# A conv and MLP-mixer kernel on one core: products of the turning tiles as pairs of 64-row halves, crossed between two banks

## The chip, the core and the metric

The kernel runs on one core of a Trainium2 chip. PE (TensorE) does the matrix products, ACT (ScalarE) and DVE (VectorE) the elementwise work, POOL and SP mostly start DMA transfers. The metric is the device time of one launch in microseconds. PE ran at its full granted clock in every slice of the profile of before.

## What is computed

Eight batches of 4096 tokens by 192 channels. A causal convolution of seven taps comes first, its taps per head softmaxed (`wsm`); then an MLP-mixer block with its two residual sums:

```python
w = np.exp(weight - weight.max(-1, keepdims=True)); w /= w.sum(-1, keepdims=True) + 1e-09
x = np.einsum('hk,bskhg->bshg', w, x_unf)                  # 7 shifted copies of x
h = np.maximum(x.transpose(0, 2, 1) @ w_tok1, 0.0) @ w_tok2    # 4096 -> 256 -> 4096 tokens
u = x + h.transpose(0, 2, 1)
out = u + np.maximum(u @ w_ch1, 0.0) @ w_ch2                   # 192 -> 1536 -> 192 channels
```

The kernel computes in fp32, mostly with operands split in a high and a low part of type fp32r (`hi`, `lo`), of which three of the four products are taken (high by high, high by low, low by high). Where fp32 itself is used a product runs as two passes.

## The kernel before

The batches form the groups [0], [1], [2, 3], [4, 5], [6, 7]. For each group the token mixing has two parts. Mix part 1 (`mix`, L929, the products at L938 or L942 to L944) sums over all 4096 tokens into two accumulator banks `ps_a0` and `ps_a1`, one for each half `kc` of the 256 mixed tokens; it runs in the background while the group before is still in its channel MLP. A planner, `bg`, keeps lists of background items with a cost, a lag and a gate, and pops them when the foreground calls `bg.fg` with the time that its last products took; while `bg.tiled` is set it pops no products. In group 1 (one batch) mix part 1 is fp32 with 192 columns, in the two-batch groups fp32r with 384.

The foreground goes tile by tile, 512 tokens of one batch each. A tile is four blocks of 128 tokens (`j`). Per tile PE does:

- **channel1** (L1261): 108 products of 64 rows by 512 columns. Two halves of the array work at a time, rows 0 to 63 on one bank and rows 64 to 127 on another: a pair. `bg.tiled` is set. ACT makes `hh` (L1315) and DVE `hl` (L1320) from each bank.
- **mix2** of the next tile, if this is a *turning* tile, the last of its tile's batches: whole 128-row products, one bank for each block j (L1109, L1110 with one batch: 384 and 192 columns; L1112 to L1114 with two: 384 columns each). DVE adds the bank to `u` (L1124, L1125 or L1128).
- **channel2**: on a turning tile `channel2`, whole rows, one bank a block, 12 steps f with an `hh` product of 384 columns (L1369) and an `hl` product of 192 (L1370), then two adds a block (L1375, L1376). On other tiles `channel2_halves` (L1337): the same in pairs of row halves, each half with its own bank, and four adds a block (L1343, L1345).
- the next tile's `u` must be turned so that the channels lie on partitions. With one batch PE transposes it (`transposed_once`, L1183, 8 transposes a tile in the middle of channel2); with two, DVE turns 32 by 32 blocks (`turn_blocks`, L1150), DMA sends them to their places (`blocks_sent`, L1201, queues of SP and POOL), ACT copies what returns (`parted`, L1213) and swaps the row halves (L1218).

Some two-batch tiles have time to be mixed a tile ahead (`spread`): their mix2 is `mix2_half` (L1139), in pairs, woven into `channel2_halves`. It is used where the background has no products left. So PE goes between pairs and whole rows at the turning tiles: pairs in channel1, whole rows in mix2 and channel2, and pairs again in the next channel1. The order of each engine is what the code writes, in the order in which `bg` pops.

## Time and profile before

| | before |
|---|---|
| median of 3 runs | 2005.86 us (2005.25 to 2006.46) |
| profiled execution, device time | 2004.13 us |
| its span, first to last instruction | 2002.4 us |
| PE busy | 1995.6 us (100%), 19007 products |
| DVE busy | 1507.4 us (75%) |
| ACT busy | 788.9 us (39%) |

Busy time counts an instruction from start to end. PE's instructions overlap in its pipeline, so how long a product takes is the step from one start to the next, not its length. In a timeline each row is the start, the length, engine, line, operation, output and inputs, shape and count; `64*128` is a half-row product, `128*128` a whole one. `[0.16 <-X]` is idle time ahead of the instruction, and what ended it.

### The profile page before, as it was taken

Reading aid. Unit: us, or ns where it says so; the run is one execution under the profiler, and the core shown is the slowest. Engines: PE = TensorE matmul, PEld = TensorE weight load, DVE = VectorE, ACT = ScalarE, POOL = GpSimd, SP = SyncE. Lnnn points to the kernel's source line nnn. Section 1 sums busy time; section 2 is a strip of 40 time slices with the busy share of each in tenths; the row PEclk is TensorE's granted clock in tenths of the full one; section 3 lists DMA queues with packets and bytes.
Section 4 is the critical chain, followed back from the end, with each engine's and each line's share of the span. In section 5 each row is a group of like instructions: output and inputs, shape, how many; then the busy total and the mean of one; then the engine's idle time right before and its main releaser. Section 6 shows DMA issues by size and latency. Waiting matters only on the chain.

```text
span 2002.4 us, 45321 instructions
## 1 busy us (share of the span) xinstructions
PE 1995.6 (100%) x19007; PEld 1852.3 (93%) x19007; DVE 1507.4 (75%) x3021; ACT 788.9 (39%) x1312; POOL 212.6 (11%) x374
## 2 busy tenths in 40 slices
PE   9999999999999999999999999999999999999999
PEld 9899999999989999999999999999999999999998
DVE  6999989999569999747898789556666666666664
ACT  7668544444343343423333433323333322333322
POOL 1000000010011101111111110111111110011110
PEclk9999999999999999999999999999999999999999
DMA  9956555553365365524346543533322222333310
GB/s 302 297 151 218 172 164 170 177 195 128 114 173 151 112 190 175 158 72 132 84 129 184 139 142 107 132 88 85 86 71 76 75 67 59 80 86 85 86 49 17
DMA packets 282080, 259.26 MB, mean 129 GB/s; under 512 B 190100, under 2 KB 231924, under 8 KB 281876
## 3 DMA queue, kind: packets, MB, share of 16 engines
q1 hardware_dynamic: 258180, 172.75, 30.6%
q0 software_dynamic: 22608, 82.97, 13.8%
q8 instruction: 150, 2.46, 0.5%
q10 hardware_dynamic: 1088, 0.64, 0.1%
q14 instruction: 54, 0.44, 0.1%
HBM read 147.25 MB, written 71.30 MB: 109 GB/s over the span
## 4 chain that ended last, share of the span: by engine, by line
PE 97%; DMA 1%; DVE 1%; POOL 0%; ACT 0%; SPq 0%; issue 0%; POOLq 0%; DVEq 0%
PE ps_x L1261 39%; PE ps_x L1337 26%; PE ps_x L1369 12%; PE ps_x L1370 5%; PE ps_x L1139 3%; PE ps_a L942 2%; PE ps_a L943 2%; PE ps_a L944 2%; PE ps_x L1109 1%; PE ps_a L938 1%; PE ps_x L1112 1%; PE ps_x L1281 1%; DMA x<-in_x_dram 1%; PE ps_x L1114 1%; PE ps_x L1113 1%; DMA dec_raw<-in_moe_w_tok_dram 1%
## 5 line engine op out<-in xcount | busy, mean ns | idle before, releaser
L1315 ACT ACTIVATE hh<-ps_x 128x512 fp32r<-128x512 f32 x752 | 408.7, 596 | 844.3 <-PE ps_x L1261 844.2
L1320 DVE SCALAR_TENSOR_TENSOR hl<-ps_x,hh 128x512 fp32r<-128x512 f32 x752 | 482.5, 685 | 177.9 <-ACT hh L1315 177.2
L1337 PE MATMUL ps_x<-w,hh 64*128 64x384 f32 x3648 | 523.0, 355 | 0.0
L1337 PE MATMUL ps_x<-w,hl 64*128 64x192 f32 x3648 | 458.4, 247 | 0.0
L1261 PE MATMUL ps_x<-other,w_hi 64*128 64x512 f32 x1728 | 448.3, 388 | 0.0
L836 DVE SCALAR_TENSOR_TENSOR xc<-raw,cw,xc 128x384 f32<-128x384 f32 (+1 forms) x768 | 388.5, 561 | 4.6 <-ACT xc L834 4.5
L1337 PEld LDWEIGHTS ps_x<-w,hl 64*128 64x128 f32 x3648 | 351.0, 188 | 1.5
L1261 PE MATMUL ps_x<-own_hi,w_hi 64*128 64x512 f32 x1440 | 346.3, 391 | 0.7 <-ACT w_hi L674 0.4
L1337 PEld LDWEIGHTS ps_x<-w,hh 64*128 64x128 f32 x3648 | 344.8, 184 | 1.5
L1261 PEld LDWEIGHTS ps_x<-other,w_hi 64*128 64x128 f32 x1728 | 315.2, 184 | 32.2 <-DVE hl L1320 0.4
L1261 PE MATMUL ps_x<-own_hi,w_lo 64*128 64x512 f32 x1440 | 341.9, 387 | 0.0
L1261 PE MATMUL ps_x<-own_lo,w_hi 64*128 64x512 f32 x1440 | 341.2, 386 | 0.0
L1369 PE MATMUL ps_x<-w,hh 128*128 128x384 f32 x1172 | 339.5, 360 | 0.0
L1370 PE MATMUL ps_x<-w,hl 128*128 128x192 f32 x1176 | 294.4, 250 | 0.0
L1261 PEld LDWEIGHTS ps_x<-own_lo,w_hi 64*128 64x128 f32 x1440 | 218.4, 184 | 25.5 <-DVE own_lo L1170 0.2
L1261 PE MATMUL ps_x<-other,w_lo 64*128 64x512 f32 x864 | 242.0, 386 | 0.0
L1261 PEld LDWEIGHTS ps_x<-own_hi,w_lo 64*128 64x128 f32 x1440 | 218.1, 184 | 25.6 <-DVE w_lo L675 0.2
L1261 PEld LDWEIGHTS ps_x<-own_hi,w_hi 64*128 64x128 f32 x1440 | 213.7, 184 | 29.4 <-issue 4.3
L1370 PEld LDWEIGHTS ps_x<-w,hl 128*128 128x128 f32 x1176 | 224.5, 191 | 0.0
L1369 PEld LDWEIGHTS ps_x<-w,hh 128*128 128x128 f32 x1172 | 220.1, 188 | 0.4 <-DVE hl L1320 0.4
L1345 DVE TENSOR_TENSOR osb<-ps_x,osb 128x192 f32<-128x192 f32 x456 | 163.1, 358 | 27.9 <-DVE osb L1345 1.8
L1261 PEld LDWEIGHTS ps_x<-other,w_lo 64*128 64x128 f32 x864 | 159.0, 184 | 16.9
(212 smaller groups left out, 2049.3 us busy)
## 6 DMA issues: line engine op xcount, KB each, us to landing
raw<-in_x_dram SPq DMA_DIRECT2D x56, 672.0 KB, 8.0
t<-t2d SPq DMA_DIRECT2D x64, 512.0 KB, 5.3
out_dram<-osb POOLq DMA_DIRECT2D x61, 384.0 KB, 4.2
xcd<-xc POOLq DMA_DIRECT2D x28, 768.0 KB, 7.7
u<-xcd SPq DMA_DIRECT2D x56, 384.0 KB, 5.5
t<-t1p SPq DMA_DIRECT2D x32, 512.0 KB, 6.1
other<-own_hi POOLq DMA_DIRECT2D x24, 384.0 KB, 3.9
other<-own_lo POOLq DMA_DIRECT2D x24, 384.0 KB, 3.8
```

What stands on the lines that cost most here:

```text
L836: nc.vector.scalar_tensor_tensor(out=dst, in0=src, scalar=cw[:, h, k:k + 1], in1=dst, op0=ALU.mult, op1=ALU.add)
L942: nc.tensor.matmul(out=ps, lhsT=wh, rhs=xh, start=a, stop=False)
L943: nc.tensor.matmul(out=ps, lhsT=wh, rhs=xl, start=False, stop=False)
L944: nc.tensor.matmul(out=ps, lhsT=wl, rhs=xh, start=False, stop=z)
L1139: nc.tensor.matmul(out=ps[:, :n], lhsT=t2[ks, kc, r, j, :], rhs=h1[ks, kc, v, :n], start=m == 0, stop=m == len(prods) - 1)
L1261: nc.tensor.matmul(out=ps, lhsT=w1[w][rows, chunks[h][c], p * P:(p + 1) * P], rhs=t[h][v][rows, c], start=n == 0, stop=n == len(prods) - 1,)
L1315: nc.scalar.activation(out=h["hh", f], in_=ps, func=AF.Relu)
L1320: nc.vector.scalar_tensor_tensor(out=h["hl", f], in0=ps, scalar=0.0, in1=f32(h["hh", f]), op0=ALU.max, op1=ALU.subtract)
L1337: nc.tensor.matmul(out=ps[:, :m], lhsT=h[part, f][ks, ts], rhs=w2[ks, f, :m], start=n == 0 and part == "hh", stop=z and part == "hl",)
L1345: nc.vector.tensor_tensor(out=osb[:, j], in0=v, in1=osb[:, j], op=ALU.add)
L1369: nc.tensor.matmul(out=ps[:, :2 * D], lhsT=h["hh", f][:, ts], rhs=w2[:, f, :], start=n == 0, stop=False)
L1370: nc.tensor.matmul(out=ps[:, :D], lhsT=h["hl", f][:, ts], rhs=w2[:, f, :D], start=False, stop=z)
```

## The change

Four kinds of products that were whole become pairs of row halves that are *crossed* between two banks: mix2 of the groups after the first (`crossed`, after's L463), mix part 1 (after's L1004), the transposes (after's L1276) and channel2 of every tile that isn't spread, save the last tile (`channel2_crossed`, after's L1474). For two blocks `one` and `two`, the first step takes rows 0 to 63 of `one` into the bank of `one`, beside rows 64 to 127 of `two` into the bank of `two`; a later step takes the other halves, so that each bank ends with the whole sum, and two adds a block suffice. The order of the steps over a tile's four blocks is `CROSSED`: (0, 1), (2, 3), then (1, 0) and (3, 2). Group 0's mix2 stays in whole rows, and so do the first tile's products and the last tile's channel2.

A bank's second half must come after its first. This is ordered through ScalarE: `signal` issues an empty ScalarE instruction (`nop`), which waits for PE's first halves, and PE's first product of the second half waits for that. The adds of mix2 come after the third and the fourth step, two blocks each; mix part 1 is split in two parts (`part` 0 and 1), taken for two `q` one after the other, with a gate on part 1. The core of the diff:

```diff
+    def signal():
+        if unsignalled:
+            relay = nc.scalar.nop(nofuse=True)
+            for key in unsignalled:
+                ordered(relay, tops_of[key][1])
+                tops_of[key] = tops_of[key][0], relay
+            unsignalled.clear()
+
+    def crossed(outs, prods, one, two, part):
+        for n, js in enumerate(zip(prods(one), prods(two))):
+            for r, (j, (m, lhs, rhs)) in enumerate(zip((one, two), js)):
+                rs = slice(r * D2, (r + 1) * D2)
+                z = len(prods(j)) - 1
+                mm = nc.tensor.matmul(
+                    out=outs[j][:, :m], lhsT=lhs(rs), rhs=rhs(rs), start=part == 0 and n == 0, stop=part == 1 and n == z
+                )
+                row_tile((id(outs), j), r, mm, part and not n, not part and n == z)
+
+    def row_tile(ps, r, mm, first, last):
+        if first and r != tops_of.get(ps, (r,))[0]:
+            ordered(mm, tops_of[ps][1])
+        if last:
+            tops_of[ps] = r, mm
+            unsignalled.append(ps)
+
+    CROSSED = ((0, 1, 0), (2, 3, 0), (1, 0, 1), (3, 2, 1))
...
-        def mix(q2, q, kc):
+        def mix(q2, q, part):
...
+            way = (q // 2 + part) % 2
+            if way != crossing["way"] and any((id(accs), kc) in unsignalled for kc in range(KC)):
+                signal()
...
+            for n in range(len(made[0])):
+                for r in range(2):
+                    kc = (r + way) % 2
+                    rs = slice(r * D2, (r + 1) * D2)
+                    m, lhs, rhs = made[kc][n]
+                    mm = nc.tensor.matmul(
+                        out=accs[kc][:, :m], lhsT=lhs(rs), rhs=rhs(rs), start=first_way and n == 0,
+                        stop=last_way and n + 1 == len(made[0]),
+                    )
+                    row_tile((id(accs), kc), r, mm, not n, n + 1 == len(made[0]))
...
+            if q % 2 == 0:
+                it.gate = lambda: 0.0 if bg.finishing or (id(accs), 0) not in unsignalled else None
@@ mix2, for the groups after the first @@
+        for one, two, part in CROSSED:
+            if not part:
+                for j in (one, two):
+                    pss[j] = ps_x.tile([P, TT], F32, name="ps_x")
+            crossed(pss, prods, one, two, part)
+            signal()
+            bg.fg(570 if nb == 1 else 1040, 2 * (660 if nb == 1 else 600) if part else 0, 200)
+            if part:
+                for j in (two, one):
+                    added(j, pss[j])
@@ transposed_once @@
+        def turned(part):
             for j in range(TJ):
-                nc.tensor.transpose(out=ps[:, j * P:(j + 1) * P], in_=cols, identity=ident)
+                for r in range(2):
+                    rs, c = slice(r * D2, (r + 1) * D2), (r + part) % 2
+                    cols = u[rs, j].rearrange("p c b d -> p (c b d)")[:, c * D2:(c + 2) * D2]
+                    mm = nc.tensor.transpose(out=pss[c][:, j * P + r * D2:j * P + (r + 1) * D2], in_=cols, identity=ident[rs, rs])
...
+    def channel2_crossed(i, h, u, osb, at, tiled):
...
+        for k, (one, two, part) in enumerate(CROSSED):
...
+            for n in range(0, 2 * NF, 8):
+                z = n + 8 == 2 * NF
+                for m in range(n, n + 8):
+                    for r, j in enumerate((one, two)):
+                        rs = slice(r * D2, (r + 1) * D2)
+                        w, lhs, rhs = made[j][m]
+                        mm = nc.tensor.matmul(
+                            out=pss[j][:, :w], lhsT=lhs(rs), rhs=rhs(rs), start=not part and m == 0,
+                            stop=part == 1 and m + 1 == 2 * NF,
+                        )
+                        row_tile((id(pss), j), r, mm, part and not m, not part and m + 1 == 2 * NF)
+                        if m % 8 == 1 and r:
+                            signal()
+                bg.fg(1140, 1320 if z and part else 0, 200)
+                if (k, n // 8) in at:
+                    at[k, n // 8]()
+            if part:
+                for j in (two, one):
+                    ps = pss[j]
+                    nc.vector.tensor_tensor(out=rows(osb[:, j]), in0=rows(ps[:, :D]), in1=tokens(u, i)[:, j], op=ALU.add)
+                    nc.vector.tensor_tensor(out=osb[:, j], in0=ps[:, D:2 * D], in1=osb[:, j], op=ALU.add)
```

PE's order at mix2 of the first two-batch tile, before. `ps_x_...` is a bank, `h1` and `t2` the operands; `[waits ...]` names the semaphores of the engines or DMA queues that an instruction waits for.

```order
L1112 MATMUL ps_x_6566<-h1_481,t2_6408 128x384 [waits DMAHW3_49,DVE_49]
L1113 MATMUL ps_x_6566<-h1_481,t2_6408 128x384
L1114 MATMUL ps_x_6566<-h1_481,t2_6408 128x384
L1112 MATMUL ps_x_6566<-h1_481,t2_6408 128x384 [waits DMAHW4_49,Activation_49]
L1113 MATMUL ps_x_6566<-h1_481,t2_6408 128x384
L1114 MATMUL ps_x_6566<-h1_481,t2_6408 128x384
L1112 MATMUL ps_x_6575<-h1_481,t2_6408 128x384 [waits DVE_49]
L1113 MATMUL ps_x_6575<-h1_481,t2_6408 128x384
```

The same place after: two banks in turn in each step, and the second halves begin with a wait on the ScalarE relay.

```order
L463 MATMUL ps_x_8496<-h1_481,t2_8338 128x384 [waits DMAHW3_49,DVE_49]
L463 MATMUL ps_x_8497<-h1_481,t2_8338 128x384 [waits DVE_49]
L463 MATMUL ps_x_8496<-h1_481,t2_8338 128x384
...
L463 MATMUL ps_x_8511<-h1_481,t2_8338 128x384 [waits DVE_49]
L463 MATMUL ps_x_8512<-h1_481,t2_8338 128x384 [waits DVE_49]
L463 MATMUL ps_x_8511<-h1_481,t2_8338 128x384
...
L463 MATMUL ps_x_8497<-h1_481,t2_8338 128x384 [waits Activation_sequencer_49]
L463 MATMUL ps_x_8496<-h1_481,t2_8338 128x384
L463 MATMUL ps_x_8497<-h1_481,t2_8338 128x384
L463 MATMUL ps_x_8496<-h1_481,t2_8338 128x384
```

Every product is now half as high and there are twice as many; the bank of a block is written in two steps, which lie one step apart.

PE's order where the background's mix part 1 stands behind a block of mix2, in a tile of the groups of two batches, before:

```order
L1112 MATMUL ps_x_8933<-h1_481,t2_8357 128x384 [waits DMAHW6_49]
L1113 MATMUL ps_x_8933<-h1_481,t2_8357 128x384
L1114 MATMUL ps_x_8933<-h1_481,t2_8357 128x384
L942 MATMUL ps_a0_6757<-xhl_8385,t1_8137 128x384
L943 MATMUL ps_a0_6757<-xhl_8385,t1_8137 128x384
L944 MATMUL ps_a0_6757<-xhl_8385,t1_8137 128x384
L942 MATMUL ps_a0_6757<-xhl_8385,t1_8137 128x384
```

and after, where mix part 1 takes the accumulators the other way round than the time before:

```order
L463 MATMUL ps_x_11249<-h1_481,t2_10656 128x384
L463 MATMUL ps_x_11250<-h1_481,t2_10656 128x384
L463 MATMUL ps_x_11249<-h1_481,t2_10656 128x384
L463 MATMUL ps_x_11250<-h1_481,t2_10656 128x384
L1004 MATMUL ps_a0_8811<-xhl_10476,t1_8839 128x384 [waits Activation_sequencer_49]
L1004 MATMUL ps_a1_8812<-xhl_10476,t1_8839 128x384
L1004 MATMUL ps_a0_8811<-xhl_10476,t1_8839 128x384
```

The first product of mix part 1 now waits for a relay that stands right behind the step of mix2 ahead of it.

PE's order in group 0's mix2, where a background product of group 1 stands behind a block, before:

```order
L1109 MATMUL ps_x_1853<-h1_481,t2s_1652 128x384 [waits Activation_49]
L1110 MATMUL ps_x_1853<-h1_481,t2s_1652 128x192
L938 MATMUL ps_a0_778<-xc0_1092,t1_942 128x192 [waits DMAHW1_49]
L938 MATMUL ps_a0_778<-xc0_1092,t1_942 128x192
L938 MATMUL ps_a1_779<-xc0_1092,t1_942 128x192 x2
L1109 MATMUL ps_x_1871<-h1_481,t2s_1652 128x384 [waits DVE_49]
L1110 MATMUL ps_x_1871<-h1_481,t2s_1652 128x192
```

and after:

```order
L1201 MATMUL ps_x_2069<-h1_481,t2s_1856 128x384 [waits Activation_49]
L1201 MATMUL ps_x_2069<-h1_481,t2s_1856 128x192
L1004 MATMUL ps_a0_778<-xc0_1092,t1_942 128x192 [waits DMAHW1_49]
L1004 MATMUL ps_a1_779<-xc0_1092,t1_942 128x192
L1004 MATMUL ps_a0_778<-xc0_1092,t1_942 128x192
L1004 MATMUL ps_a1_779<-xc0_1092,t1_942 128x192
L1201 MATMUL ps_x_2084<-h1_481,t2s_1856 128x384 [waits DVE_49]
L1201 MATMUL ps_x_2084<-h1_481,t2s_1856 128x192
```

Mix part 1's products are half-row pairs on both accumulators there, with whole rows ahead and behind.

## Rows read from the trace of the kernel before

**Rows 1.** The page: busy time of each engine, and the chain's shares by engine.

```profile
PE 1995.6 (100%) x19007; PEld 1852.3 (93%) x19007; DVE 1507.4 (75%) x3021; ACT 788.9 (39%) x1312; POOL 212.6 (11%) x374
...
PE 97%; DMA 1%; DVE 1%; POOL 0%; ACT 0%; SPq 0%; issue 0%; POOLq 0%; DVEq 0%
```

**Rows 2.** PE's timeline from channel1 to channel2_halves, 598 us: start, length.

```profile
598.29 0.39 PE L1261 MATMUL ps_x<-own_lo,w_hi 64*128 64x512 f32 x1
...
598.52 0.33 PE L1337 MATMUL ps_x<-w,hh 64*128 64x384 f32 x2
...
598.78 0.36 PE L1337 MATMUL ps_x<-w,hh 64*128 64x384 f32 x2
...
599.06 0.36 PE L1337 MATMUL ps_x<-w,hh 64*128 64x384 f32 x2
```

**Rows 3.** PE's timeline where channel1 passes into whole-row mix2, 568 us.

```profile
567.80 0.39 PE L1261 MATMUL ps_x<-own_lo,w_hi 64*128 64x512 f32 x2
568.12 0.44 PE L1112 MATMUL ps_x<-h,t 128*128 128x384 f32 x1
...
568.56 0.34 PE L1114 MATMUL ps_x<-h,t 128*128 128x384 f32 x1
```

**Rows 4.** PE's timeline where whole-row channel2 passes into channel1, 586 us.

```profile
585.46 0.36 PE L1369 MATMUL ps_x<-w,hh 128*128 128x384 f32 x1
...
585.75 0.36 PE L1369 MATMUL ps_x<-w,hh 128*128 128x384 f32 x1
...
586.12 0.49 PE L1261 MATMUL ps_x<-own_hi,w_hi 64*128 64x512 f32 x1
```

**Rows 5.** Groups of PE by line and shape: count | busy us, mean ns.

```profile
L1112 PE MATMUL ps_x<-h,t 128*128 128x384 f32 x80 | 27.9, 349 | 0.0
...
L938 PE MATMUL ps_a<-xc,t 128*128 128x192 f32 x128 | 23.8, 329 | 0.0
...
L1183 PE MATMUL ps_x<-ident,u 128*128 128x128 f32 x112 | 14.5, 272 | 0.0
...
L1109 PE MATMUL ps_x<-h,t 128*128 128x384 f32 x64 | 20.0, 366 | 0.0
```

**Rows 6.** PE's timeline at a one-batch tile's transposes, 110 us.

```profile
110.00 1.03 PE L1183 MATMUL ps_x<-ident,u 128*128 128x128 f32 x8
```

**Rows 7.** PE's weight loads at the first pairs of channel1, 586 us.

```profile
586.12 0.18 PEld L1261 LDWEIGHTS ps_x<-own_hi,w_hi 64*128 64x128 f32 x1 [0.16 <-issue]
586.12 0.18 PEld L1261 LDWEIGHTS ps_x<-other,w_hi 64*128 64x128 f32 x1
```

**Rows 8.** PE's timeline at fp32 products of mix part 1, 160 us.

```profile
160.39 1.49 PE L938 MATMUL ps_a<-xc,t 128*128 128x192 f32 x8
...
161.88 0.25 PE L1110 MATMUL ps_x<-h,t2s 128*128 128x192 f32 x1
```

**Rows 9.** ACT's and PE's timelines where one waits for the other.

```profile
54.16 0.59 ACT L1169 CAST own_hi<-ps_x 128x512 fp32r<-128x512 f32 x1
...
54.80 0.50 PE L1261 MATMUL ps_x<-own_hi,w_hi 64*128 64x512 f32 x2 [0.26 <-ACT own_hi L1169]
...
598.71 1.09 ACT L1315 ACTIVATE hh<-ps_x 128x512 fp32r<-128x512 f32 x2 [0.95 <-PE ps_x L1261]
```

**Rows 10.** Waits by engine and line: total us, times, longest us.

```profile
ACT xc L834 <- DVE xhl L926: 20.4, 3, 9.7
```

**Rows 11.** DVE's and PE's timelines where channel2 follows mix2, one batch, 330 us.

```profile
329.41 1.28 DVE L1320 SCALAR_TENSOR_TENSOR hl<-ps_x,hh 128x512 fp32r<-128x512 f32 x2
...
330.42 0.36 PE L1369 MATMUL ps_x<-w,hh 128*128 128x384 f32 x1
```

**Rows 12.** ACT's and PE's timelines before channel1 of a tile turned by DMA.

```profile
640.00 1.48 ACT L1218 CAST other<-own_hi 64x1536 fp32r<-64x1536 f32 x1
...
642.51 0.49 PE L1261 MATMUL ps_x<-own_hi,w_hi 64*128 64x512 f32 x1
```

More of the change, by code (lines that the diff above doesn't have):

```diff
@@ L44, in __init__ @@
         self.tiled = False
+        self.finishing = False
         self.pe = 0.0
@@ L436, in mix1_done, with ordered @@
             )
+    tops_of, unsignalled = {}, []
+    def ordered(later, sooner):
+        tc.add_manual_dep(
+            later.ins, sooner.ins.name,
+            mybir.DependencyInfo(mybir.DependencyClass.Sync, mybir.DependencyReason.DATA), reason="row tiles of one bank",
+        )
[22 more added lines that the diff above has]
+    CROSSED = ((0, 1, 0), (2, 3, 0), (1, 0, 1), (3, 2, 1))
     def mix1_accs():
@@ L988, in prepare, with multiply @@
                 mixing.append(Item(lambda: split_lo(*a), cost=MJ * nb * D / 0.96 + 150, lag=500 + 350 * nb))
-        def multiply(*a):
+        def multiply(part, *a):
             q2, q = a
@@ L1030, in stage1 @@
                     prepare(q2, q + k)
-                for k in range(2):
-                    multiply(q2, q + k)
+                for part in range(2):
+                    for k in range(2):
+                        multiply(part, q2, q + k)
         def finish():
@@ L1129, in mix2 @@
                 turn_blocks(uj, turned, j)
+        if not gi:
+            for j in range(TJ):
+                ps = mix1_accs()[j] if at_once and q and j < 2 else ps_x.tile([P, TT], F32, name="ps_x")
+                whole = slice(0, P)
+                made = [] if at_once else prods(j)
+                for k, (m, lhs_of, rhs_of) in enumerate(made):
+                    nc.tensor.matmul(
+                        out=ps[:, :m], lhsT=lhs_of(whole), rhs=rhs_of(whole), start=k == 0, stop=k + 1 == len(made)
+                    )
+                for kc in range(KC if at_once else 0):
+                    at_once_mm(ps, kc, j)
+                bg.fg(570 if nb == 1 else 1040, 660 if nb == 1 else 600, 200)
+                added(j, ps)
+            return
+        pss = {}
+        for one, two, part in CROSSED:
+            if not part:
+                for j in (one, two):
[6 more added lines that the diff above has]
+                    added(j, pss[j])
     def mix2_half(t2, u, j, turned):
@@ L1190, in moved @@
             nc.scalar.copy(out=own[k][low, ND - 1], in_=f32(own[k][high, ND - 2]))
-        moved(0)
-        return [(own, own, [range(ND), [(c + 1) % ND for c in range(ND)]])], lambda: moved(1)
+        return [(own, own, [range(ND), [(c + 1) % ND for c in range(ND)]])], turned, lambda: moved(1)
     def blocks_sent(z, place, queues=(nc.sync, nc.gpsimd)):
@@ L1629, in conv_mixer_kernel @@
                 else:
-                    if ahead:
-                        if turn and pairs:
-                            made = []
-                            channel2(i, h, u, osb, half[1], ((half[1][0], 7), lambda: made.extend(parted(other[:, 1], other))))
-                            abc = made
-                        elif turn:
-                            channel2(i, h, u, osb, half[1], ((half[1][0], 7), rest))
-                        else:
-                            product2(i, h, u, osb, half[1])
-                    else:
+                    if not ahead:
                         made = []
```

138 lines of the change are left out of this document (89 added, 49 removed).

## The prediction

> **What bounds the kernel now.** I read the page's busy times first, then the chain of waits, then PE's timeline where the work changes form, then the weight loads, then the other engines where PE could come to wait for them. PE is busy 1995.6 of 2002.4 us, and the chain that ends last is PE for 97% [rows 1]. So the kernel is one long row of products; PE's idle time in the whole span is some 7 us. DVE's 1507 us and ACT's 789 us lie beside it. An edit can win in two ways only: fewer or shorter products, or less time lost between them. It loses by anything that makes PE stand.
>
> **What is removed: switches of row form.** The order of PE's instructions has 52 changes between 64-row pairs and whole 128-row products in the kernel before, and 24 in the changed one. What one costs is read where a tile passes from channel1 to mix2, and where it goes back.
> - To whole rows: channel1's pairs start 0.23 us apart (598.29 to 598.52 [rows 2]). The first whole product starts 0.32 us after the last pair (+0.09), and lasts 0.44 us where the third lasts 0.34 (+0.10) [rows 3].
> - Back to pairs: one hh and one hl product together take 0.29 us; the last such two take 0.37 us up to the next pair (+0.08) [rows 4], and that pair lasts 0.49 us instead of 0.39 (+0.10) [rows 2, 4].
>
> A round trip thus costs 0.37 us. Tiles whose whole-row mix2 and channel2 become pairs: 80 products of L1112 at 8 a tile are 10 tiles; 64 of L1109 on batch 1 are 8 tiles [rows 5]. 18 round trips go: -6.7 us. On group 0 mix2 stays whole, so its round trip merely ends sooner: nothing. Four round trips are added, where products of the next group's mix part 1, now pairs, stand inside that whole-row mix2: +1.5. **Sum of the switches: -5.2 us.** Nothing covers a switch, so all of it is on the path.
>
> **What becomes pairs at the same price.** Channel2's pairs start 0.28 us apart for hh and hl together, whole rows 0.29 [rows 2, 4]: a pair of row halves, for two blocks, costs as much as a whole product for one, and does as much. So channel2's whole products, and the fp32r ones of mix2 and of mix part 1, are costed at nothing; the 0.01 of difference is the rounding of the rows. Four two-batch tiles go from the halves of before (L1139, L1337) to the crossed form, since the planned work of the next group lasts longer: pairs for pairs, nothing.
> The transposes are bound by their weight loads: eight last 1.03 us, one 0.27, so they start 0.109 us apart [rows 5, 6]. There are 8 a tile over 14 tiles. The change makes eight pairs a tile of them. Two halves' loads start at the same time, 586.12 and 586.12 [rows 7], so eight pairs last as long as eight whole ones: nothing. If the halves' loads went in turn, it would be 14 x 8 x 0.109 = +12.2 us.
> The Trainium skill, page "TensorE: Matmul & The Clock Gate", section "LDWEIGHTS (loading the stationary operand)", has a rule that speaks against halves: a load takes as long as it has columns, and half the rows save nothing. With loads in turn the sum would have the 12.2 us on top; with loads that overlap, as the rows show, it has nothing, and I give the rule no weight beyond the rival on fp32 below.
>
> **fp32 products of mix part 1 (group 1).** 64-row fp32 pairs don't occur before. Whole, eight passes take 161.88 - 160.39 - 0.20 = 1.29 us, 0.161 each (0.20 is what a 384-column product of mix2 takes before the one behind it) [rows 8]; all 128 passes are 20.6 us [rows 5]. If the two halves run beside each other but start in order, a stretch of pairs ends skewed by half a pass to a pass: 25 stretches at 0.08 to 0.16 us are 2 to 4 us. Without a skew it is nothing; if the halves don't overlap at all, +20.6. I take +2.5: the fp32r pairs, the nearest rows, do overlap [rows 2].
>
> **What is added: ordering by relays.** The second half of a bank waits for an empty ScalarE instruction, which waits for the bank's first half; 133 products wait so. Worked out from the products that stand between, at the pace above, 68 of them (channel2) have 3.26 us of cover, 14 (transposes) 1.13, those of mix2 0.58 to 2.7. A relay needs 0.03 us from PE's end to ACT (598.29 + 0.39 = 598.68, ACT at 598.71 [rows 2, 9]) and 0.05 back (a cast ends at 54.16 + 0.59 = 54.75, the product that it frees starts at 54.80 [rows 9]). All of these hide it as long as ACT is free. Eight have no cover: there mix part 1 swaps its banks right behind a step of mix2 (seven) or of its own (one), and the relay waits for that step's last products too, 0.05 to 0.09 us of work ahead. PE then runs empty: a product's 0.34, the relay's 0.03 + 0.05, some 0.03 for the empty instruction, and the 0.10 of a first pair [rows 4], less the 0.17 that a product takes anyway: 0.38, and with a little overlap 0.37 each. **8 x 0.37 = +3.0 us.** Ends: 1.6 (0.2 each, if only the hop shows) and 7.7 (a cast of 0.59 [rows 9] ahead of each).
> ACT executes in order, so a relay also stands behind whatever ACT waits for, and PE behind it, and behind PE everything. Three casts of L834 waited 20.4 us for DVE, one of them 9.7 [rows 10]; that is longer than the 3.26 us of cover. Most relays stand ahead of such a cast in ACT's order. I take +1 for it, ends 0 and 6.
>
> **DVE.** Channel2's halves need four adds a block, the crossed form two; 160 adds fewer. PE seldom waits for DVE, so this is worth at most a part of PE's 7 idle us: -0.7, ends 0 and -3.
>
> **Banks.** Crossed mix2 takes four banks in its first two steps, and channel2 then takes two at once. The second of these is freed by hl of channel1's last pair: in the tile read this ends at 329.41 + 1.28 = 330.69, and channel2 begins at 330.42 [rows 11]. PE would stand 0.27 us. For the eight one-batch tiles that is 2.2 at most if all were as late; I take **+1.7**, ends 0 and 3.
>
> **The turned blocks.** Where the next tile goes through DMA, mix2's adds and turns begin after its third step, not its first: two steps of six products at 0.17 us, 2.1 us later at the start, and about 1.5 at the end, since DVE was behind already. Queued behind the later turns are SP's and POOL's sends of the blocks, ACT's copies of what comes back, and channel1. At the tightest tile the copy that channel1 needs ends at 640.00 + 1.48 = 641.48 and channel1 starts at 642.51, 1.03 us of slack [rows 12]. 1.5 later, with PE 0.3 sooner, gives a stall of 0.8 there and little elsewhere: **+1**, ends 0 and 3.
>
> **Sum:** -5.2 + 2.5 + 3.0 + 1.0 - 0.7 + 1.7 + 1.0 = +3.3 us; with all terms at one end -6.6 or +18.5. The profiled execution took 2004.13 us (its span of 2002.4 and 1.7 around it), 1.7 below the median of 2005.86; the sum is a difference and holds for both. The terms that have cover (ACT, banks) are more likely smaller than larger, so I forecast +2 on the median, **2008 us**: within 0.2%, which is 4 us and about what a measurement of this kernel can tell from no change.
>
> **Rivals.**
> 1. Faster. Relays, banks and skew all hide: -5.2 - 0.7 gives 2000.0 us. For it: PE waits almost nowhere now, and most covers are longer than a hop. Against it: the eight relays that have no cover.
> 2. Slower, by fp32. The row halves of fp32 passes don't run beside each other: mix part 1 costs 20.6 more, the transposes, fp32 too, 12.2; with the rest of the sum (0.8) 2005.9 + 33.6 = 2039.5 us, or 2027 with the products alone. It decides by whether the second half's pass starts beside the first or at its end. No row of before shows an fp32 pair; against it stand the loads side by side [rows 7].
> 3. Slower, by ACT. Relays queue behind casts that wait. One behind a 9.7 us wait costs 9.7 - 3.3 = 6.4 us; two give 2005.9 + 3.3 + 12.8 = 2022 us, one 2015.6. It decides from a wait of 3.3 us ahead of a relay.
> 4. The edit doesn't do what it says. The time at a switch belongs not to the row form but to the first use of new operands, and stays: 2005.9 + 3.3 + 5.2 = 2014.4 us. Against it: channel1 passes into channel2's pairs at the usual 0.23 [rows 2].
>
> **How the numbers follow.** Forecast 0.45, rival 1 0.25, rival 2 0.10, rival 3 0.12, rival 4 0.08. Faster by over 0.2%: rival 1 and a little of the forecast, 0.28. Slower: rivals 2 to 4 and the forecast's upper end, less the lower ends of 3 and 4, 0.32. Within: the rest, 0.40. The forecast's own range is 2002 to 2013. The whole range leaves out rival 2 and the far end of 3: 1998.5 to 2018 us.
>
> **What would show it.** Right: 25 stretches of one row form in PE's timeline; channel1 into mix2 0.23 apart; eight gaps of some 0.5 us before a product of mix part 1 that follows mix2, put down to ScalarE; tenths of a us of waiting of PE for DVE's hl at the banks; one stall of about 1 us before channel1 near 640. Wrong: mix part 1's fp32 halves 0.16 us apart each rather than each pair (rival 2); waits of PE of several us for ScalarE (rival 3); gaps that stay at channel1's end though the form doesn't change (rival 4).

## The result

| | before | after |
|---|---|---|
| median | 2005.55 us (4 runs) | 2019.36 us (2016.99 to 2020.78, 4 runs) |
| profiled execution, device time | 2004.13 us | 2019.74 us |
| its span | 2002.4 us | 2018.0 us |
| DVE busy | 1507.4 us | 1442.8 us |

The ratio is 1.0068, 95% interval [1.005, 1.0085]: the change is slower, by 13.8 us on the medians and 15.6 us on the two spans. The forecast was 2008 us, which it called about as much as no change, and its range ended at 2018.

### The profile after

The page's busy times and its chain by engine, as in [rows 1]:

```profile
PE 2000.2 (99%) x22495; PEld 1867.9 (93%) x22495; DVE 1442.8 (71%) x2861; ACT 791.0 (39%) x1312; POOL 212.4 (11%) x374
...
PE 45%; DVE 2%; DMA 1%; SPq 1%; ACT 0%; issue 0%; ACTq 0%; DVEq 0%
```

PE isn't busy for 17.8 us of the span (before 6.8). The chain that ends last is put down to PE for 45%, where [rows 1] had 97%; its shares add up to 49% only, and no other engine has over 2%, so this line says little here. What PE waits for, in total us, times, longest:

```profile
PE ps_x L1359 <- ACT other L1316: 3.4, 3, 2.0
PE ps_a L1004 <- DVE xhl L965: 2.1, 1, 2.1
PE ps_a L1004 <- ACTq L451: 1.5, 2, 1.3
PE ps_x L1474 <- ACTq L451: 1.5, 1, 1.5
```

L1316 is ACT's swap of the row halves of a block that came back by DMA (L1218 before); L451 is the relay. None of the four waits is in the trace of before. They add up to 8.5 us only; the rest is small steps and stretches at half clock, which count as busy. So I took each tile from its first channel1 product to the next tile's, subtracted its products at the pace of undisturbed tiles, and compared the two kernels. Tiles are named by the time at which they begin. After 1500 us they agree to 0.01 us a tile. Ahead of that some tiles win, by 6.3 us in sum. The losers are the turning tile of 514 to 560 us (+4.6), the turned tile of 709 to 740 (+5.2), the relay at 115 (+1.6), the fp32 stretch of 147 to 287 (+1.6, the four added round trips), and a dozen of 0.4 to 2.1.

**The stall at 551.** PE's timeline of after, the end of group 1's tiles, where mix part 1 of the group after must finish:

```profile
551.26 0.44 PE L1004 MATMUL ps_a<-xhl,other 64*128 64x384 f32 x2 [0.39 <-ACT xhl L961]
553.85 1.62 PE L1004 MATMUL ps_a<-xhl,other 64*128 64x384 f32 x10 [2.14 <-DVE xhl L965]
```

Each `q` is now used twice, in part 0 and in part 1, for two `q` in turn, so both buffers of `xhl` are held until both parts are done, and DVE makes the next operand too late. That is a reading of the code; the runs below test it. The leftover at the group's end is 132 half products, 120 halves' worth before.

**The stall at 709.** PE and ACT of after, then DVE and SP of after, then DVE, SP and ACT of before at the same tile:

```profile
709.15 0.49 PE L1359 MATMUL ps_x<-own_hi,w_hi 64*128 64x512 f32 x1 [0.24 <-ACT own_hi L1311]
711.69 0.79 PE L1359 MATMUL ps_x<-other,w_hi 64*128 64x512 f32 x1 [2.05 <-ACT other L1316]
...
708.48 1.66 ACT L1311 CAST own_hi<-other 128x512 fp32r<-128x512 f32 x3 [6.52 <-DMA other<-own_hi]
710.16 1.47 ACT L1316 CAST other<-own_hi 64x1536 fp32r<-64x1536 f32 x1
```

```profile
687.55 5.38 DVE L875 SCALAR_TENSOR_TENSOR xc<-raw,cw,xc 128x384 f32<-128x384 f32 x10
692.84 0.56 DVE L1192 TENSOR_TENSOR u<-ps_x,u 128x384 f32<-128x384 f32 x1
...
697.20 6.46 SPq L1299 DMA_DIRECT2D other<-own_hi  x8
```

```profile
685.16 0.55 DVE L1128 TENSOR_TENSOR u<-ps_x,u 128x384 f32<-128x384 f32 x1
...
690.79 5.11 SPq L1201 DMA_DIRECT2D other<-own_hi  x8
...
697.89 1.66 ACT L1213 CAST own_hi<-other 128x512 fp32r<-128x512 f32 x3 [9.59 <-DMA other<-own_hi]
```

Mix2's adds begin 7.7 us later (692.84, 685.16), but 4.7 of that is the tile's own later start (673.21, 668.53); 3.0 are the change's third step and the ten taps of the convolution that stand ahead of them on DVE. Counted from the tile's start the sends begin 1.7 us later, ACT's copies 5.9, since the blocks take 4.2 us longer from the first send until they are back. And channel1 is due 3.2 us sooner, because 60 halves of mix part 1 stand in this tile where before has 96. Together this uses up the slack of 6 us that channel1 had there (the copies it needs done at 701.06, channel1 at 707.25 in before).

**What a stall costs beyond itself.** PE by windows: length and busy us (products), granted clock, DMA share, GB/s.

```profile
551.00:554.00 3.00, 0.59 (x4) 1.00 0.23 54
554.00:558.00 4.00, 3.90 (x26) 0.57 1.11 326
558.00:566.00 8.00, 8.00 (x80) 1.00 0.24 98
...
712.00:715.00 3.00, 3.00 (x16) 0.55 1.20 327
```

Behind each of the two stalls of about 2.5 us the granted clock is down at its 1.2 GHz level for some 3 us (the 0.57 and 0.55 are means over windows that also hold some time at the full clock), and PE does half the work in them: some 1.5 us more each.

### The profile page after: what moved, and what is told of

Read it like the earlier page. It is cut to its first block, busy times and chain, and to the rows that moved or that the text cites. A ratio compares the mean times of both kernels' runs of the same rounds, so it can differ in the third digit from the quotient of the medians.

```text
span 2018.0 us, 52240 instructions
## 1 busy us (share of the span) xinstructions
PE 2000.2 (99%) x22495; PEld 1867.9 (93%) x22495; DVE 1442.8 (71%) x2861; ACT 791.0 (39%) x1312; POOL 212.4 (11%) x374
## 5 line engine op out<-in xcount | busy, mean ns | idle before, releaser
L1474 PE MATMUL ps_x<-w,hh 64*128 64x384 f32 x4000 | 589.1, 358 | 0.5 <-DVE hl L1418 0.3
L1474 PE MATMUL ps_x<-w,hl 64*128 64x192 f32 x4008 | 541.3, 247 | 0.1
L1474 PEld LDWEIGHTS ps_x<-w,hl 64*128 64x128 f32 x4008 | 452.4, 188 | 1.2 <-DVE hl L1418 0.8
L1474 PEld LDWEIGHTS ps_x<-w,hh 64*128 64x128 f32 x4000 | 448.0, 184 | 2.9 <-DVE hl L1418 1.2
L1359 PE MATMUL ps_x<-own_hi,w_hi 64*128 64x512 f32 x1440 | 361.7, 390 | 1.3 <-ACT w_hi L713 0.4
L1359 PE MATMUL ps_x<-own_hi,w_lo 64*128 64x512 f32 x1440 | 357.0, 387 | 0.0
L1359 PE MATMUL ps_x<-own_lo,w_hi 64*128 64x512 f32 x1440 | 356.0, 387 | 0.0
L1435 PE MATMUL ps_x<-w,hh 64*128 64x384 f32 x1920 | 276.6, 354 | 0.0
L1359 PEld LDWEIGHTS ps_x<-own_lo,w_hi 64*128 64x128 f32 x1440 | 233.0, 184 | 20.4 <-DVE own_lo L1260 0.2
L1359 PEld LDWEIGHTS ps_x<-own_hi,w_lo 64*128 64x128 f32 x1440 | 233.2, 184 | 20.1 <-DVE w_lo L714 0.2
L1359 PEld LDWEIGHTS ps_x<-own_hi,w_hi 64*128 64x128 f32 x1440 | 227.8, 184 | 21.8 <-DVE hl L1418 0.9
L1435 PE MATMUL ps_x<-w,hl 64*128 64x192 f32 x1920 | 244.5, 247 | 0.0
L1435 PEld LDWEIGHTS ps_x<-w,hl 64*128 64x128 f32 x1920 | 190.1, 188 | 0.7
L1435 PEld LDWEIGHTS ps_x<-w,hh 64*128 64x128 f32 x1920 | 187.2, 184 | 0.9
L1487 DVE TENSOR_TENSOR osb<-ps_x,u 128x192 f32<-128x192 f32 x168 | 58.9, 351 | 96.7 <-PE ps_x L1474 96.5
(196 smaller groups left out, 1998.5 us busy)
```

Of the source, the lines that this page charges most:

```text
L1359: nc.tensor.matmul(out=ps, lhsT=w1[w][rows, chunks[h][c], p * P:(p + 1) * P], rhs=t[h][v][rows, c], start=n == 0, stop=n == len(prods) - 1,)
L1435: nc.tensor.matmul(out=ps[:, :m], lhsT=h[part, f][ks, ts], rhs=w2[ks, f, :m], start=n == 0 and part == "hh", stop=z and part == "hl",)
L1474: mm = nc.tensor.matmul(out=pss[j][:, :w], lhsT=lhs(rs), rhs=rhs(rs), start=not part and m == 0, stop=part == 1 and m + 1 == 2 * NF,)
L1487: nc.vector.tensor_tensor(out=rows(osb[:, j]), in0=rows(ps[:, :D]), in1=tokens(u, i)[:, j], op=ALU.add)
```

## The experiments

**Theory**, from the traces: what the prediction counted as gain is there, and the loss is order. Mix part 1 in two parts holds `xhl`; the planner fills DVE with taps ahead of mix2's adds; and relays stand behind ACT's waits. **Rivals**: the adds that come later are the loss by themselves; the order of mix part 1's parts is; the half-row products are dearer than they look; or the end of whole rows is what costs. Each run was timed beside runs of the kernel before; where two medians are given, the second is theirs.

**Two parts of the change alone.** The kernel before with mix2's adds taken two and two, after blocks 2 and 3:

```diff
+            late.append((j, ps))
+            if gi and j < 2:
+                bg.fg(570 if nb == 1 else 1040, 0, 200)
+                continue
+            bg.fg(570 if nb == 1 else 1040, (2 if gi else 1) * (660 if nb == 1 else 600), 200)
+            for j, ps in (late[:2] if j == 2 else late[2:]) if gi else late[-1:]:
+                added(j, ps)
```

> The kernel before, with whole rows everywhere, and only one thing of the change: mix2's adds come in twos, blocks 0 and 1 after the third block's products, 2 and 3 after the fourth's. Theory A (the time is lost because the turned blocks are late: DVE does conv taps ahead of the adds, and channel1 of the next tile waits): slower by 2 to 6 us, 2008 to 2012 us, with a stall of PE before a channel1 near 707 us. Theory B (the time is lost because mix part 1 is ordered and gated in two parts): no change, 2004.5 to 2006.5 us. Theory C (relays behind ACT): no change either.

2006.69 us beside 2004.82, ratio 1.0011 [1.0002, 1.0021]: 1.9 us. PE at the tile of [rows 12]:

```profile
642.30 0.50 PE L1271 MATMUL ps_x<-own_hi,w_hi 64*128 64x512 f32 x1
643.34 0.50 PE L1271 MATMUL ps_x<-other,w_hi 64*128 64x512 f32 x1 [0.54 <-ACT other L1228]
```

The stall of 0.8 that the prediction worked out there is there (1.04 between pairs instead of 0.23), and a second one of 1.0 us at 778, where channel1 waits for DVE's add. The later adds alone are a seventh of the loss. The tile that stalls at 709 in the changed kernel doesn't stall here, though the same ten taps stand ahead of its adds. DVE, ACT and PE:

```profile
683.68 5.37 DVE L836 SCALAR_TENSOR_TENSOR xc<-raw,cw,xc 128x384 f32<-128x384 f32 x10
688.97 0.55 DVE L1115 TENSOR_TENSOR u<-ps_x,u 128x384 f32<-128x384 f32 x1
...
700.52 1.66 ACT L1223 CAST own_hi<-other 128x512 fp32r<-128x512 f32 x3 [11.38 <-DMA other<-own_hi]
...
708.09 0.50 PE L1271 MATMUL ps_x<-own_hi,w_hi 64*128 64x512 f32 x1
```

The adds begin 19.8 us into the tile, as late as in the changed kernel (19.6; before 16.6), and the copies 31.4 us into it (35.3; before 29.4). With 96 halves of mix part 1 in the tile channel1 is due at 38.9, and the later adds take 2 of the 6 us of slack, not all of it.

The kernel before with mix part 1's items in the order of the two parts, whole rows kept:

```diff
-                for k in range(2):
-                    multiply(q2, q + k)
+                for part in range(2):
+                    for k in range(2):
+                        multiply(part, q2, q + k)
```

> The kernel before, whole rows, and only the order of mix part 1's items: for two q, both accumulators' halves as part 0 of q and q+1, then part 1 of q and q+1 (before: both of q, then both of q+1). No relay, no gate. Theory B: operand buffers are held longer, so loads and splits come later; slower by 2 to 5 us, 2007.5 to 2010.5 us, with PE waiting for DVE's xhl near the end of group 1 (550 us). Theory A and C: no change, 2004.5 to 2006.5 us.

2005.43 us, ratio 1.0004 [0.9994, 1.0013]: no difference. The order alone, without halves, relays and gate, costs nothing that shows.

**Mix2's adds ahead of the taps.** The changed kernel, but the planner places no background work of DVE in mix2's first three steps:

```diff
-            bg.fg(570 if nb == 1 else 1040, 2 * (...) if part else 0, 200)
+            bg.fg(570 if nb == 1 else 1040, 2 * (...) if part else 0, 200 if one == 3 else -1e6)
```

> The changed kernel, but while mix2's first three steps run the planner places no background work on DVE, so that the adds don't stand behind conv taps. Theory A: the stall before channel1 at 709 us (2.7 us and 1.6 of lower clock) goes, and part of those near 1027, 1060 and 1206 us: 2012 to 2015 us. Theory B: 2017 to 2021 us, the stall near 551 us stays and the taps merely come later.

2014.71 us beside 2004.82, ratio 1.0048 [1.0033, 1.0063]: 9.9 us over the kernel before, where the changed kernel is 13.8 over its own. The stall before channel1 at 709 is gone; another stands ahead of the same channel1, at 716. PE, DVE, and ACT's copies:

```profile
716.28 1.97 PE L1004 MATMUL ps_a<-xhl,t 64*128 64x384 f32 x10 [4.66 <-ACTq L451]
...
696.09 4.28 DVE L875 SCALAR_TENSOR_TENSOR xc<-raw,cw,xc 128x384 f32<-128x384 f32 x8
700.29 0.55 DVE L1192 TENSOR_TENSOR u<-ps_x,u 128x384 f32<-128x384 f32 x1
...
713.57 1.66 ACT L1311 CAST own_hi<-other 128x512 fp32r<-128x512 f32 x3 [6.12 <-DMA xcd<-xc]
715.26 1.47 ACT L1316 CAST other<-own_hi 64x1536 fp32r<-64x1536 f32 x1
```

The relay for mix part 1 stands behind the three copies and the first swap, which wait 6.1 us for a DMA, and PE behind the relay. That is rival 3 in person, only behind L1311's copies and not L834's casts. What made the first stall go isn't what the edit was meant to do: only the first two adds come sooner, eight taps now stand ahead of the last two, and the copies begin 37.3 us into the tile, 2.1 later than in the changed kernel. But the tile has its 96 halves of mix part 1 again. So of the 3.9 us won, the share of the adds' order isn't shown.

**Both parts of a `q` side by side**, so that `xhl` is free after one `q`:

```diff
-            way = (q // 2 + part) % 2
+            way = (q + part) % 2
...
-                for part in range(2):
-                    for k in range(2):
+                for k in range(2):
+                    for part in range(2):
```

> The changed kernel, but part 0 and part 1 of mix part 1 follow each other for each q (the accumulators are swapped at every q), so a q's operands are free sooner, at the price of about twice as many waits for relays (each 0.2 to 0.3 us where it has no cover). Theory B: the stall near 551 us (2.4 + 0.6 us and 1.6 of lower clock) goes: 2013 to 2017 us. Theory A: no gain, 2019 to 2023 us by the added relays.

2019.86 us (2016.90 to 2023.67; the trace is of a launch of 2023.67), ratio 1.0077 [1.0061, 1.0093]: 15.0 over the kernel before, the changed one 13.8. The stall at 551 shrank to 0.81 and 0.26 us more than the pace, with no fall of the clock. So the order of the parts has a large share in it, but not all: in e12, e16 and e23 below, which have this order for that group and e2's adds as well, PE still waits 1.73 us for DVE's `xhl` there (2.13 in e2). Also, the banks are swapped twice as often, with more relays inline, and waits at turned tiles grew:

```profile
PE ps_x L1359 <- ACT other L1316: 4.2, 4, 2.0
```

**No relay for the accumulators while ACT's copies are queued** (e2 with that; then also with both parts of a `q` together in the first two-batch group):

```diff
...
+        keys = [k for k in unsignalled if force or not (bg.copying and k in acc_keys)]
...
```

> As e2_adds_first, and from the moment at which ACT's copies of the returned blocks are queued until the tile's end no relay is made for mix part 1's accumulators (their second part then waits for the next tile). Theory C (PE waits for a relay that stands in ACT's order behind copies which wait for a DMA): the wait of 4.7 us near 716 us, with the 2 to 3 us of lower clock after it, goes: 2006.5 to 2009.5 us. If the relay only takes the place of some other lateness: 2012 to 2015 us, with the stall at the next channel1.

> As e9_relay_clear, and for the group of batches 2 and 3 part 0 and part 1 of mix part 1 follow each other for each q, so that each of the two xhl buffers is free sooner when the rest of that group is finished near 551 us; some 8 more relays without cover, 0.2 to 0.3 us each. Theory B in its narrow form (buffers held by two q at the end of the group): the stall of 2.4 + 0.5 us near 551 us and the lower clock after it shrink to 1 to 2 us: 2 to 3 us less than e9_relay_clear, 2004 to 2007 us. Otherwise as e9_relay_clear or 2 us more.

2028.47 us (2022.42 to 2036.11), ratio 1.0117 [1.009, 1.0145], and 2027.27, ratio 1.011 [1.0094, 1.0127], beside 2004.23: 24.2 and 23.0 over the kernel before. The wait at 716 is gone (0.49 us at that tile's channel1 is left), yet both are 13 to 14 us slower than e2: a miss. Without the relay the gate lets fewer products through (48 halves a tile where e2 has 96), and what is left over comes at the group's end, where nothing covers it. The trace of the first is of a launch of 2022.42 us, so it holds less than the whole loss. PE, 1044 us:

```profile
1045.01 1.14 PE L1007 MATMUL ps_a<-xhl,t 64*128 64x384 f32 x10 [0.55 <-DVE xhl L967]
1048.12 3.37 PE L1007 MATMUL ps_a<-xhl,t 64*128 64x384 f32 x18 [1.97 <-DMA t<-t1p]
```

**Mix part 1 in whole rows again**, the rest as changed:

```diff
-            for n in range(len(made[0])):
-                for r in range(2):
-                    kc = (r + way) % 2
...
+            ms = slice(kc * P, (kc + 1) * P)
+            for j in range(MJ):
```

> The changed kernel with mix part 1 as before it: whole 128-row products, its own order, no gate, no relay; channel2, mix2 and the transposes stay crossed. The row form now changes 126 times, 102 more than in the changed kernel. If a round trip costs 0.37 to 0.42 us wherever it is: +19 to +21 us, less what the relays, the gate and the late finish of mix part 1 cost (up to 10 us): 2028 to 2037 us. If the price doesn't belong to the row form: 2009 to 2016 us.

2027.36 us beside 2004.23, ratio 1.0112 [1.0097, 1.0127]: 23.1 over. This prices the switches a second time. It has 63 round trips, which cost 25.95 us in its trace (0.41 each); the kernel before has 26 at 11.37 us (0.44), the changed one 12 at 5.47 us (0.46). 51 more trips cost 20.5 us, and the kernel is only 9.3 us slower than the changed one (23.1 less 13.8): but for the switches, whole rows in mix part 1 would be some 11 us ahead, though they bring a stall of their own (4.4 us over the pace at 653). The stall at 551 isn't there, and neither is the one at 709, though mix2's adds begin 20.9 us into that tile and ten taps stand ahead of them here too. So a round trip costs what the prediction said or a little more, and mix part 1 as crossed halves (their order, gate, relays and finish together) is where most of the loss lies, the stall at 709 included; this run doesn't part them.

**ACT's copies queued later**, at step (3, 0) of channel2 instead of (2, 1), on top of e2; then with both parts together in the first two-batch group:

```diff
-                        at[2, 1] = lambda: made.extend(parted(other[:, 1], other))
+                        at[3, 0] = lambda: made.extend(parted(other[:, 1], other))
```

> As e2_adds_first, and ACT's copies of the returned blocks are queued a third of channel2's last step in, instead of halfway through its third step, so that the relays of mix part 1 stand ahead of them; mix part 1's products lie on the same tiles as in e2_adds_first and in the kernel before (96 halves on each of eight tiles). Theory C: the wait of 4.7 us for a relay near 716 us, with 2 us of lower clock behind it, goes and nothing takes its place: 2006.5 to 2009.5 us. If the turned blocks are late there anyway: 2011 to 2015 us, with the stall at the next channel1.

> As e15_copies_later, and for the group of batches 2 and 3 the two parts of mix part 1 follow each other for each q, so that xhl's two buffers are free one q at a time when the group is finished near 555 us. Theory B in its narrow form: the stall of 2.4 + 0.5 us there and the lower clock behind it shrink to about 2 us, at the price of some 6 relays without cover at 0.22 us: 1.5 to 3 us less than e15_copies_later, 2004 to 2007 us. Otherwise the same as e15_copies_later or 1 us more.

2030.97 us, ratio 1.0124 [1.0107, 1.0141], and 2026.92, ratio 1.0109 [1.0094, 1.0124], beside 2005.12: 25.9 and 21.8 over. The first is a miss in direction, 16 us slower than e2. The relays stood behind the copies more often, not less:

```profile
PE ps_a L1004 <- ACTq L451: 12.3, 4, 5.6
```

The mechanism is the one named, a relay behind copies in ACT's queue, but moving the copies back made it worse. The second is 4.0 us better than the first; its stall near 554 is 2.06 us between two products instead of 2.58.

**The relay on SyncE** while the copies are queued, with e2's adds and both parts together in that group:

```diff
...
-            relay = nc.scalar.nop(nofuse=True)
+            relay = (nc.sync if bg.copying else nc.scalar).nop(nofuse=True)
```

> As e16_both, but ACT's copies of the returned blocks are queued where the changed kernel has them (halfway through channel2's third step), and the relays made between there and the tile's end stand on SP instead of ACT: the same order of PE, another queue for some ten relays. Theory C: the waits for a relay behind copies that wait for a DMA (4.7 us near 716 us in e2_adds_first, 12 to 13 us in the two kernels with later copies) go: 2004.5 to 2008.5 us. If the queue doesn't matter (the first halves themselves or the operands are late): 2011 to 2014 us. If SP's own waits for free buffers take their place: over 2014 us.

2012.89 us (2010.43 to 2016.03) beside 2004.59, ratio 1.0044 [1.0027, 1.0061]: 8.3 over. e2 was 9.9 over (2011.77 to 2016.21), so the difference between the two isn't clear of noise; the waits are. From SP's relays PE waits 0.2 us in all:

```profile
PE ps_a L1005 <- SPq L452: 0.2, 1, 0.2
```

From the tile that begins at 733 us in the kernel before, the lag behind it falls from 8.9 us to 6.1 at the end of the span's turning tiles: 2.8 us won. What is lost lies ahead of that.

**Crossing only where it paid.** The kernel before up to group 1 (mix part 1 of groups 0 to 2 and the transposes included), the crossed form with e2's adds and SP's relays for the tiles of batches 2 to 7:

```diff
+                if gi <= 2:
+                    for k in range(2):
+                        multiply_whole(q2, q + k)
+                    continue
...
-                    mix2(*nxt, *loaded, turned=z)
+                    mix2(*nxt, *loaded, turned=z, crossing=gi >= 2)
```

> The kernel before as it stands for the tiles of groups 0 and 1 and for mix part 1 of groups 0 to 2 (whole rows, its order, whole transposes); the crossed form with relays only for the tiles of groups 2 to 7 and mix part 1 of groups 3 on, with mix2's adds ahead of the background as in e2_adds_first and the relays on SyncE while ScalarE's copies are queued as in e23_relay_on_sp. In e23 each turning tile from number 21 on carried next to no excess where the kernel before carries 0.31 to 0.44 us, some 3 us in all, and its losses lay in tiles 2 to 20. Theory 1 (a crossed tile saves its round trip wherever nothing waits, and the losses belong to the early tiles): 2001 to 2004 us where the kernel before gives about 2004.8, so 0.5 to 3 us faster. Theory 2 (the stalls at tiles 18 and 20 belong to the crossed form itself, not to a leftover of the early tiles): they stay, some 1.2 and 2.9 us, and the time is 2004.5 to 2006. Theory 3 (e23's gain late was paid for by work done early): excess of 0.4 us a tile comes back late, 2006 to 2009.

2004.95 us (11 runs) beside 2005.31 (15), ratio 0.9997 [0.9988, 1.0006]: no difference. Theory 2 it is. From 612 to 1386 us its tiles win 3.8 us in sum, and two lose 3.3, those that begin at 642 (+0.98) and 707 (+2.32). PE and DVE at the second:

```profile
714.89 0.47 PE L1393 MATMUL ps_x<-own_hi,w_hi 64*128 64x512 f32 x1 [0.93 <-DVE osb L1522]
...
708.71 5.37 DVE L876 SCALAR_TENSOR_TENSOR xc<-raw,cw,xc 128x384 f32<-128x384 f32 x10
714.01 0.35 DVE L1521 TENSOR_TENSOR osb<-ps_x,u 128x192 f32<-128x192 f32 x1
714.39 0.36 DVE L1522 TENSOR_TENSOR osb<-ps_x,osb 128x192 f32<-128x192 f32 x1
```

Crossed channel2 frees its last two banks together at the end of the tile, and the planner put ten taps ahead of the adds that free them. One number moves them:

```diff
-                bg.fg(1140, 1320 if z and part else 0, 200)
+                bg.fg(1140, 1320 if z and part else 0, 200 if k < 3 or tiled else -3000)
```

> h1_late_groups with one number changed: in the last step of the crossed channel2 of a turning tile the planner places background work of DVE only if DVE is 3 us behind PE, so that the last two adds into osb stand ahead of most of the convolution's taps (2 taps ahead of them at the tightest tile, before 10). In h1 two turning tiles gained 0.98 and 2.32 us of waiting over the kernel before (the ones that begin at 642 and 707 us; at the second channel1 waits 0.93 us for DVE's add into osb, which stands behind ten taps of 5.4 us), while all others together won some 3.7. Theory 1 (that wait is DVE's order and nothing else): both stalls go, 2001 to 2003 us where the kernel before gives about 2005, ratio 0.9982. Theory 2 (the tight tile's data come late anyway, through DMA and ScalarE's copies): the stall at 714 stays at 0.9 or more and the time is that of h1, 2005. Theory 3 (the taps that are put off make channel1's hl late): the stalls move to channel2's first products, 2004 to 2006.

2005.52 us (11 runs) beside 2005.09 (15), ratio 1.0002 [0.9993, 1.0011]: no difference either; theory 3. The adds are done by 710.98, and the wait for them is gone. But the taps put off now stand ahead of channel1's `hl`, for which PE's weight loads wait:

```profile
710.90 4.32 DVE L876 SCALAR_TENSOR_TENSOR xc<-raw,cw,xc 128x384 f32<-128x384 f32 x8
715.13 1.28 DVE L1452 SCALAR_TENSOR_TENSOR hl<-ps_x,hh 128x512 fp32r<-128x512 f32 x2
...
715.87 0.18 PEld L1393 LDWEIGHTS ps_x<-own_hi,w_hi 64*128 64x128 f32 x1 [0.55 <-DVE hl L1452]
```

The 707 tile loses 1.52 instead of 2.32, and three others lose 0.15 to 0.32 that lost nothing. At those tiles DVE has too much to do for either order. No version here beats the kernel before.

## Why the prediction failed

By its own terms, each measured as what PE's products start late by over the pace, in the trace of after:

| term | predicted | measured | |
|---|---|---|---|
| switches | -5.2 | -5.9 | 26 round trips to 12, 11.37 to 5.47 us |
| transposes | 0 | -4 | eight pairs 0.44 us, eight whole ones 0.79, on 14 tiles |
| fp32 pairs | +2.5 | 0 | halves start 7 ns apart, 0.16 us a pair pass |
| eight inline relays | +3.0 | +2.6 | seven at 0.37, the eighth is in the finish's row |
| relays behind ACT's waits | +1 | +4.1 | 115.53: 1.6, 900.73: 1.4, four of 0.1 to 0.4 |
| banks | +1.7 | +2 | 0.42 at three places, 0.2 to 0.5 on other tiles |
| turned blocks | +1 | +9 | 5.2 at 709, 1.0 at 646, 1.2 at 1206, several of 0.5 |
| mix part 1's finish | no term | +4.7 | the stall at 551 and its half clock |
| sum | +3.3 with DVE's -0.7 | +12.5 | the spans differ by 15.6; some 3 us in small steps aren't placed |

**Right.** The switch price, within 0.7 us: the mechanism and the size. So is the price of channel2's pairs: crossed channel2 takes 13.63 us, as `channel2_halves` did. The Trainium skill, page "TensorEngine Tiling (Array Packing)", section "Key Properties", says that changing the tiling mode drains TensorE; the three counts of round trips above agree in that every change takes time, and put 0.41 to 0.46 us on a change there and back. Rival 2 fell, by the fp32 pairs of mix part 1 in after:

```profile
161.04 0.82 PE L1201 MATMUL ps_x<-h,t2s 128*128 128x384 f32 x4
161.78 0.92 PE L1004 MATMUL ps_a<-xc,t 64*128 64x192 f32 x8
```

Four pairs, eight records, last 0.92 us, where eight whole passes lasted 1.49 [rows 8]: a pair follows 0.162 us behind the pair ahead, as a whole pass did. Rival 4 fell with the switches. An inline relay looks and costs as it was drawn: PE's product of mix part 1 starts 0.44 us after the last of mix2's instead of 0.17, and the pair behind it 0.28 us later instead of 0.17, which makes 0.37:

```profile
754.91 1.04 PE L463 MATMUL ps_x<-h,t 64*128 64x384 f32 x10
756.06 1.15 PE L1004 MATMUL ps_a<-xhl,t 64*128 64x384 f32 x10
```

**Wrong, and lucky: transposes.** They were "bound by their weight loads", so "eight pairs last as long as eight whole ones: nothing". They take little over half as long. PE of after at four pairs, of before at eight whole ones, each with the product behind:

```profile
471.65 0.40 PE L1276 MATMUL ps_x<-ident,u 64*128 64x64 f32 x8
471.87 0.41 PE L1474 MATMUL ps_x<-w,hh 64*128 64x384 f32 x2
...
139.49 1.03 PE L1183 MATMUL ps_x<-ident,u 128*128 128x128 f32 x8
140.28 0.42 PE L1369 MATMUL ps_x<-w,hh 128*128 128x384 f32 x1
```

Four pairs take 0.22 us, so the eight of a tile 0.44; the step behind them is 0.05 us longer than elsewhere, once more often than before, which leaves 0.3 us a tile. A half moves 64 columns (64x64), a whole one 128, and weight loads of 0.14 us each, in both kernels, follow each other at 0.06 us here and 0.11 there: the loads weren't what bound them. A gain of some 4 us that no term had kept the miss smaller.

**Wrong in size: relays behind ACT.** The step "a relay also stands behind whatever ACT waits for" was right and taken at +1, by the casts of L834. The worst case came from other casts, in a tile with transposes; PE and ACT:

```profile
115.53 0.73 PE L1474 MATMUL ps_x<-w,stage 64*128 64x384 f32 x6 [1.52 <-ACTq L451]
...
113.29 0.67 ACT L202 ACTIVATE dec_top<-dec_raw 128x512 f32<-128x512 f32 x1 [2.48 <-DMA dec_raw<-in_moe_w_tok_dram]
113.86 0.60 ACT L243 CAST t2s<-dec_top 128x512 fp32r<-128x512 f32 x1
114.37 1.06 ACT L1282 CAST own_hi<-ps_x 128x512 fp32r<-128x512 f32 x2
```

ACT came out of a wait for DMA with four instructions to do, and the relay stood behind them. Rival 3's times, 2015.6 and 2022 us, lie around the measured one, but by chance: its waits of several us aren't in the changed kernel, where the longest wait for a relay is 1.52.

**Wrong: turned blocks.** The step that failed is "1.5 later, with PE 0.3 sooner, gives a stall of 0.8 there and little elsewhere". It moves everything behind the adds by the adds' own delay, and reads the slack of each tile with mix part 1's products where before has them. The delay itself was nearly right: into the tile of 707 us the adds begin 3.0 us later and end 1.8 later, where 2.1 and 1.5 were worked out, and the tile named has its stall (0.8 in b_adds, 1.0 in after). But at 707, where the slack was 6 us and which the prediction hadn't read, the blocks took 4.2 us longer to come back, and the tile, with 60 halves of mix part 1 instead of 96, ended 3.2 us sooner. b_adds and e4, with as late adds and the same ten taps but mix part 1 as before, have no stall there. Why the blocks come back later isn't shown: SP's eight sends take 6.46 us instead of 5.11, and the convolution's stores stand right behind POOL's sends, but no run takes the one from the other.

**Wrong: mix part 1 costed by its products alone.** That its two parts hold `xhl` twice as long, that gate and planner spread its products over more tiles (36 to 84 halves on twelve, where before has 96 on eight), and that what is left over comes at a group's end uncovered, had no term. e3 shows the first in part; e9 and e4 bear on the rest, where the 11 us of e4 are worked out and not measured by themselves. The terms' upper ends together were +18.5, which holds the measured +13.8; the range of 1998.5 to 2018 left these ends out.

## What to carry to other kernels

An edit that leaves PE's products alone but delays when another engine's result is asked for has to be read in that engine's new order, at every tile, before its cost is written down. The slack of a tile is no property of that tile alone: here the planner moved over a third of mix part 1's products off the tile that needed them as cover. Ordering through a third engine cost 0.37 us where nothing covered it, and up to that engine's wait where something was queued ahead (5.6 us behind ACT's copies in e15_copies_later, 0.2 on SyncE's queue). And a saving of 0.4 us a tile is worth having only on tiles where no other engine is near its limit.

## What the runs showed of the hardware

Two row halves in fp32 run side by side as the fp32r ones do, 7 ns apart, which no row of before showed.

A stop of PE can cost twice. Behind the idle time of 2.14 us at 551 and that of 0.24 and 2.05 at 709 the granted clock was at its 1.2 GHz level for some 3 us, behind that of 4.66 in e2_adds_first for some 5 us, with products twice as far apart. Behind shorter ones it mostly stayed at 1.00: after the 1.52 us at 115 and the 1.30 us at 900 in the changed kernel, and in e23_relay_on_sp after the waits of 1.7 and 1.4 us at 555 and 719. But the length of the stop alone doesn't decide: in e9_relay_clear the clock was at 0.50 behind the 1.97 us at 1048 shown above, and at 1.00 behind a wait of 1.95 us:

```profile
1537.86 2.39 PE L1007 MATMUL ps_a<-xhl,t 64*128 64x384 f32 x20 [1.95 <-DMA t<-t1p]
```

Half transposes of 64 columns start 0.06 us apart in each half of the array, whole ones of 128 columns 0.11, with weight loads of the same length.
